# A linear-attention and MLP block on one core: the second pair's w2 and attention as one product by seven products, its output transposed and summed on GpSimd

## The chip, the cores and the metric

The kernel runs on one core of a Trainium2 chip. A core has TensorE for matrix products (PE in the profile; PEld is its loading of weights), VectorE (DVE), ScalarE (ACT), GpSimd (POOL) and SyncE (SP), which here only issues DMA transfers. SBUF is the core's memory with 128 partitions, PSUM the memory into which TensorE writes; GpSimd computes from and to SBUF. The metric is the device time of one execution in microseconds (us), the median of the runs.

## The reference

Everything is float32, 2048 tokens of 512 channels, 32 heads of 16, 1376 hidden channels.

```python
xn = layernorm(x)                                  # over the 512 channels
q, k, v = split(xn @ wqkv)                         # [512, 1536]
pq, pk = phi(q), phi(k)                            # phi(t) = where(t > 0, t + 1, exp(t)) + 1e-6
kv, z = einsum("bhsd,bhse->bhde", pk, v), pk.sum(tokens)
attn = (pq @ kv) / (pq . z + 1e-6) @ wo            # wo: [512, 512]
h = relu(xn @ w1 + b1) ** 2                        # w1: [512, 1376]
out = x + attn + h @ w2 + b2                       # w2: [1376, 512]
```

## The kernel before, in words

**Products in three passes.** Each float32 operand is split into a high part (a copy by ACT, which rounds to float32r) and a low part (what is left, a subtraction by DVE of two SBUF operands: `split`, L122, `rest_of`, L125). A product is three matmuls: high x high, high x low, low x high (`PASSES`, `three`, L133). All tiles have 128 partitions; a matmul's weights are 128 x 128 and it streams 512 or 256 columns.

**Tokens.** The 16 tiles of 128 tokens make four blocks of 512 tokens. A first loop over the tiles normalises x, transposes it and builds k and the sum over tokens (`kx`, L398). From it comes `m`, the matrix by which phi(q) goes into the output (kv times wo). Then the loop `for n in range(2)` (L1060) takes the token blocks in two pairs: blocks 3 and 2 (t1, t2) in the first pair, 1 and 0 in the second.

**Places.** Per pair, q and w1 are worked off in seven "places" (`order`: two for q, five for w1), each of which makes 2 x 128 output channels for both blocks of the pair. A place is a 2 x 2 product of blocks made with seven block products instead of eight (`product`, L498: six matmuls of 512 columns each): the operands on the weights' side are the quarters A11, A12, A22 and the sums S1 to S4 of quarters (`chunk_sums`, L736, on DVE), split into parts by `chunk_split` and `last_split` into the tiles `aop`; on the tokens' side they are the transposed x (`xs`) and its differences (`T`). The banks A, before, B and C of PSUM hold the block products; ACT copies and DVE adds bring them together.

**After a place.** For w1 the results go through relu (L486) and a square to a hidden tile, which is split (`hidden_2`) and multiplied by its 128 rows of w2 (`mlp_2`, 12 matmuls) for t1 in between the products of the next places, and for t2 after the places. For q, `steps_of` turns phi(q) and divides by its sum on ACT and DVE. In the first pair attention is added with `add_attention` (12 matmuls for 128 tokens), in the second by `Seven`: block products of 256 columns (L1046) with sums made by DVE. The last 96 hidden channels go as two 128-row matmuls and one 32-row matmul for a tile of tokens (`last_2`, `quarters_2`).

**Output.** The output of 128 tokens is a bank of 512 columns; DVE adds it to the tile `res` (L1178), which holds x and, through an adding DMA on POOL's queue, b2; SP stores it.

**Order.** The program's order on each engine is as the code records it; how many of the waiting steps are taken at a point of a place is in tables (`AT`, `AE`, `TM`). SP's queue is worked off in order. Rings set reuse: tag "p" has six tiles of 512 columns, tag "raw" six for loads.

Of the kernel before, what the change touches and what calls it, by code (L numbers as in the profile page):

```python
# [10 lines left out]
OP = mybir.AluOpType  # L11
# [7 lines left out]
def kernel(  # L19
# [400 lines left out]

    def steps_of(t, j, done=False, parts=False):
# [8 lines left out]
        def weighted():  # L430
            pz = w512(f"pz{t}_{j}", "p", 6)
            tiles.append(pz)
            nc.scalar.activation(pz, o, AF.Identity, bias=zc[:, 1, j:j + 1], scale=zc[:, 0, j:j + 1])  # L433

        def sums():
            pt = w512(f"pt{t}_{j}", "p", 6)
            den = small.tile([P, H], F32, name=f"dt{t}_{j}", tag="den")
            nc.vector.transpose(blocks(pt), blocks(tiles[0]))
            nc.vector.tensor_reduce(den, heads_of(pt), axis=AX.X, op=OP.add)
            tiles.append(den)  # L440
# [534 lines left out]
    def matrix_sums(stage):  # L975

        t = [two(f"mr{r}") for r in range(2)]
        for r in range(2):
            nc.gpsimd.dma_start(t[r], md[:, 2 * r:2 * r + 2])
# [7 lines left out]
        def high(x, h, to, at):  # L987
            copy("act", h.bitcast(F32R), x)
            nc.gpsimd.dma_start(mtd[0][:, to, at], h)

        def low(x, h, to, at):
            nc.vector.tensor_tensor(out=x.bitcast(F32R), in0=x, in1=h, op=OP.subtract)
            nc.gpsimd.dma_start(mtd[1][:, to, at], x)
# [6 lines left out]
    class Seven:  # L1000

        def __init__(self, t, pairs=range(2)):
            self.t = t
            self.at = [slice(r * BT // 2 + pairs[0] * P, r * BT // 2 + (pairs[-1] + 1) * P) for r in range(2)]
            self.o = [[q[t][:, 2 * c:2 * c + 2, at] for c in range(2)] for at in self.at]

        def sums_o(self):

            (a11, a12), (a21, a22) = self.o
            return [lambda: self.op(a22, a21, a22, OP.add), lambda: self.op(a21, a11, a21, OP.subtract),  # L1010
                    lambda: self.op(a11, a22, a11, OP.subtract), lambda: self.op(a12, a12, a11, OP.subtract)]

        def op(self, o, x, y, how):
            nc.vector.tensor_tensor(out=o, in0=x, in1=y, op=how)

        def load_m(self):

            self.mt = both("mt", ("xs0h", "xs0l"))
            for o, src in zip(self.mt, mtd):
                nc.gpsimd.dma_start(f32(o), src)  # L1020

        def parts(self, src, to, order):

            highs, lows = [], []
            for c, at in order:
                h, l, x = (a[:, 2 * c:2 * c + 2, at] for a in (*to, src))
                highs.append(lambda h=h, x=x: copy("act", h, x))
                lows.append(lambda h=h, l=l, x=x: rest_of(l, x, h))
            return highs, lows

        def parts_o(self):

            self.s = both(f"so{self.t}", ("xs1h", "xs1l"))
            one, two = self.at
            return self.parts(q[self.t], self.s, ((1, one), (0, one), (0, two), (1, two)))

        def run(self, ps, left, right, e, first=False):

            c, r = left[1:]
            for i in range(2):  # L1040
                for n, (u, v) in enumerate(PASSES):
                    at = slice(r * (BT // 2) + e * P, r * (BT // 2) + (e + 1) * P)
                    a = aT[self.t, 2 * c + i][:, u, at] if left[0] == "a" else self.s[u][:, 2 * c + i, at]
                    w, k, z = right
                    b = (m if w == "m" else self.mt)[v][:, 2 * k + i, z]
                    nc.tensor.matmul(ps, lhsT=a, rhs=b, start=first and i == 0 and n == 0, stop=False,  # L1046
                                     skip_group_check=True)

        def into(self, ps, k, a):

            r = res[self.t, k][:, a]
            if a != LO and a != HI:
                r, ps = r.rearrange("p (a z) -> p a z", a=2), ps[:, None, :].to_broadcast([P, 2, D // 2])
            nc.vector.tensor_tensor(out=r, in0=ps, in1=r, op=OP.add)

    ALL = slice(0, D)

    last = TB - 1
    res = {}
    for n in range(2):  # L1060
        t1, t2 = NB - 1 - 2 * n, NB - 2 - 2 * n
        x1, x2 = xsb
        tag = "acc" if n else "ps"

        order = [("q", 0), ("w", 0), ("q", 1), *(("w", k) for k in range(1, NP))]
        NO = len(order)

        AT = (((0, 0, 0, 0, 0, 0, 0, 0, 0),
# [14 lines left out]
               (0, 0, 0, 0, 0, 0, 0, 2, 0)))[n]  # L1083
        AE = ((3, 1, 2, 3, 5, 2, 0, 1, 4, 5, 2),
              (2, 3, 2, 2, 0, 0, 0, 0, 0, 0, 0))[n]
        TM = {(1, 0): 4, (1, 4): 2, (1, 6): 1, (2, 4): 2, (3, 7): 1, (3, 0): 1, (4, 7): 1} if n else {}

        def matrix_step(p, at):
            do(m_sums, TM.get((p, at), 0))

        steps = {t1: [], t2: []}
        r2 = [work.tile([P, k, 512], F32, name=f"r2{u}{n}", tag=f"r{u}") for u, k in zip("abc", (4, 4, 3))]
        waiting = [*range(NF - 2, -1, -1), NF - 1]
        r2 = {f: r2[k // 4][:, k % 4] for k, f in enumerate(waiting)}
        m_sums = matrix_sums([r2[f] for f in waiting[:4]]) if n else []

        def last_units(rz):
            nc.scalar.activation(rz, rz, AF.Square)
            sz, rests = hidden_last(f"sz{n}", rz)

            def packed():
                lqs.append(quarters(f"sz{n}", rz, sz[0], work, "heads"))

            return sz, rests, packed

        lqs = []

        if n == 0:

            more()  # L1110
            pz2 = bank("pz0b")
            plain_1(pz2, z, x2)
            more()

            rz = r2[1]
            relu(rz, pz, NF - 1)
            relu(r2[NF - 1], pz2, NF - 1)
            do(extra, 2)
            values()
            do(extra, len(extra))  # L1120
        else:
            w2next = []
            pz = bank(f"pz{n}", "acc")
            plain_1(pz, z, x1)
        q.update({t1: four(f"q{t1}", "r2"), t2: four(f"q{t2}", "r1")})
        attention_places("r3", "r0")
        w = load_1(*order[1])
        s = {}
        if n:
            rz = w512(f"rz{n}", "p", 6)  # L1130
            relu(rz, pz, NF - 1)
            sz, sz_rests, packed = last_units(rz)
            sz_rests()
            packed()

        w2order = [NF - 1, *range(NF - 1)]

        def next_2(t):

            do(w2next, 2 - highs.pop(0))  # L1140
            if t + 1 < NF and (n == 0 or t >= TB - 1):
                f = w2order[t + 1]
                w2next.extend(piece_2(f, place(f)))

        def high_2():
            do(w2next)
            highs[0] = 1

        highs = [0] * NF
        if n:  # L1150
            next_2(0)


        banks = [bank(f"b{n}_{k}") for k in range(4)]
        t5, biased = None, []

        def load_res(t):
            for k in range(2):
                r = two(f"res{t}_{k}")
                i = t * TB + 2 * k  # L1160
                nc.sync.dma_start(r, xf[i * P:(i + 2) * P, :].rearrange("(i p) d -> p i d", i=2))
                for i in range(2):
                    res[t, 2 * k + i] = r[:, i, :]
                biased.append(r)

        def add_bias():

            def to(r):
                for i in range(2):
                    nc.gpsimd.dma_start(r[:, i], b2[None, :].partition_broadcast(P), accum_op=OP.add)  # L1170

            todo = [lambda r=r: to(r) for r in biased]
            biased.clear()
            return todo
# [420 lines left out]
```

## Time and profile before

| | us |
|---|---|
| median of 3 runs (407.48 to 408.0) | 407.62 |
| the profiled execution's span | 406.3 |
| PE busy | 401.3 |
| DVE busy | 329.2 |
| ACT busy | 273.3 |
| POOL busy | 57.3 |
| DMA moved | 55.31 MB, mean 136 GB/s |

The span runs from the first to the last instruction of the profiled execution; the time of a run also holds what lies around it. Busy time of an engine is the union of its instructions. A matmul's row in the profile is longer than the distance to the next one, because matmuls overlap; what one costs in a chain of them is the distance. "PEclk" is the clock that TensorE was granted, in tenths, DMA "share" the mean busy share of the 16 DMA engines.

### The profile page before, as it was taken

How to read it: one execution, taken by the hardware profiler on the slowest of the kernel's cores; microseconds unless marked ns; L12 is line 12 of the kernel's file. 1: busy time of each engine (PE TensorE's matmuls, PEld its weight loads, DVE VectorE, ACT ScalarE, POOL GpSimd, SP SyncE). 2: the span in 40 equal slices, each digit the busy share in tenths (PEclk: the TensorE clock that was granted, in tenths of full speed). 3: DMA queues.
4: the chain of work that ended last, by engine and by line, in shares of the span. 5: the costliest groups of instructions: out<-in, count | busy, mean ns of one | idle time of the engine just before them, and what ended most of it. 6: DMA issues, size and time to landing. Idle time of an engine off the chain costs nothing.

```text
span 406.3 us, 5887 instructions
## 1 busy us (share of the span) xinstructions
PE 401.3 (99%) x2011; PEld 334.1 (82%) x2011; DVE 329.2 (81%) x603; ACT 273.3 (67%) x478; POOL 57.3 (14%) x93
## 2 busy tenths in 40 slices
PE   8999999999999999999999999999999999999996
PEld 7888888888788888888878888888888888888895
DVE  5886666497898999988349998598989688989983
ACT  5777777456788789887728751578678857957430
POOL 5444333220000000030000300102200013000300
PEclk9999999999999999999999999999999999999999
DMA  5857656820463231291563912824331739306512
GB/s 210 275 166 230 208 157 205 241 45 0 121 193 80 77 103 27 85 224 29 186 231 124 227 38 91 231 53 129 122 113 52 207 110 305 53 34 224 105 26 105
DMA packets 48623, 55.31 MB, mean 136 GB/s; under 512 B 8593, under 2 KB 31377, under 8 KB 48082
## 3 DMA queue, kind: packets, MB, share of 16 engines
q1 hardware_dynamic: 44994, 45.50, 36.4%
q0 software_dynamic: 3520, 9.44, 9.9%
q8 instruction: 16, 0.26, 0.3%
q14 instruction: 13, 0.11, 0.1%
q10 hardware_dynamic: 80, 0.00, 0.0%
HBM read 40.90 MB, written 12.85 MB: 132 GB/s over the span
## 4 chain that ended last, share of the span: by engine, by line
PE 97%; DMA 1%; DVE 1%; ACT 0%; issue 0%
PE b L498 33%; PE acc L133 32%; PE pk L378 11%; PE kx L398 11%; PE acc L1046 2%; PE acc L509 2%; PE pz L133 1%; PE x L1046 1%; PE xl L1046 1%; DMA x<-in_A_x_dram 1%; PE b L133 1%; PE pz0b L133 1%; PE pt L310 0%; PE yl L1046 0%; PE y L1046 0%; PE acc L516 0%
## 5 line engine op out<-in xcount | busy, mean ns | idle before, releaser
L133 PE MATMUL acc<-w2r,s 128*128 128x512 f32 x477 | 113.0, 390 | 0.0
L133 PEld LDWEIGHTS acc<-w2r,s 128*128 128x128 f32 x477 | 89.3, 188 | 19.0 <-issue 0.7
L498 PE MATMUL b<-T,aop 128*128 128x512 f32 x336 | 83.5, 390 | 0.0
L498 PEld LDWEIGHTS b<-T,aop 128*128 128x128 f32 x336 | 63.0, 188 | 13.9 <-ACT t L114 0.8
L398 PE MATMUL kx<-pk,tok 128*128 128x512 f32 x192 | 46.0, 390 | 0.0
L398 PEld LDWEIGHTS kx<-pk,tok 128*128 128x128 f32 x192 | 36.0, 188 | 7.6 <-ACT pk L114 0.2
L1170 POOL DMA_DIRECT2D res<-in_B_b_dram x16 | 14.4, 1038 | 173.6 <-DVE S L736 85.9
L498 PE MATMUL b<-xs0h,aop 128*128 128x512 f32 x112 | 36.9, 391 | 0.0
L114 ACT ACTIVATE aop<-S 128x512 fp32r<-128x512 f32 x28 | 17.5, 624 | 13.1 <-DVE S L736 13.1
L359 POOL TENSOR_TENSOR tok<-xp,tok 128x512 fp32r<-128x512 f32 x15 | 19.8, 1320 | 39.8 <-ACT tok L114 39.8
L498 PEld LDWEIGHTS b<-xs0h,aop 128*128 128x128 f32 x112 | 21.0, 188 | 4.4
L125 DVE TENSOR_TENSOR w2r<-r,w2r 128x512 fp32r<-128x512 f32 (+2 forms) x35 | 23.8, 683 | 0.7 <-ACT w2r L114 0.6
L114 ACT ACTIVATE w2r<-r 128x512 fp32r<-128x512 f32 x32 | 19.6, 618 | 6.1 <-PE acc L133 4.7
L122 DVE TENSOR_TENSOR aop<-S,aop 128x512 fp32r<-128x512 f32 x28 | 19.3, 689 | 4.5 <-ACT aop L114 4.1
L498 PE MATMUL b<-xs0l,aop 128*128 128x512 f32 x56 | 21.8, 389 | 0.0
L122 DVE TENSOR_TENSOR s<-c,s 128x512 fp32r<-128x512 f32 x20 | 13.6, 689 | 7.6 <-ACT s L114 7.4
L498 PE MATMUL b<-xs1h,aop 128*128 128x512 f32 x56 | 19.5, 389 | 0.0
L114 ACT ACTIVATE T<-Tf 128x512 fp32r<-128x512 f32 x16 | 9.5, 625 | 14.4 <-DVE Tf L679 14.3
L114 ACT ACTIVATE c<-b 128x512 f32<-128x512 f32 x28 | 16.4, 585 | 2.8 <-PE b L498 2.6
L433 ACT ACTIVATE pz<-q,zc 128x512 f32<-128x512 f32 x16 | 12.9, 808 | 6.3 <-DVE q L419 6.3
L1178 DVE TENSOR_TENSOR res<-acc,res 128x512 f32<-128x512 f32 x16 | 10.5, 688 | 7.9 <-PE acc L133 5.1
L369 ACT ACTIVATE k<-pk 128x512 f32<-128x512 f32 x16 | 9.5, 593 | 9.7 <-PE pk L378 9.5
(265 smaller groups left out, 853.8 us busy)
## 6 DMA issues: line engine op xcount, KB each, us to landing
r<-in_B_w_dram SPq DMA_DIRECT2D x49, 256.0 KB, 3.5
res<-in_A_x_dram SPq DMA_DIRECT2D x8, 512.0 KB, 4.7
res<-in_B_b_dram POOLq DMA_DIRECT2D x16, 256.0 KB, 5.8
out_dram<-res SPq DMA_DIRECT2D x15, 256.0 KB, 2.1
via<-xp SPq DMA_DIRECT2D x5, 512.0 KB, 2.6
xg<-via SPq DMA_DIRECT2D x20, 128.0 KB, 2.8
xTd<-t SPq DMA_DIRECT2D x8, 256.0 KB, 3.4
x<-in_A_x_dram SPq DMA_DIRECT2D x4, 512.0 KB, 4.4
```

What stands on the lines that cost most here:

```text
L114: nc.scalar.activation(o, i, AF.Copy, bias=bias)
L122: ENG[el].tensor_tensor(out=l, in0=src, in1=f32(h), op=OP.subtract)
L125: nc.vector.tensor_tensor(out=l, in0=src, in1=f32(h), op=OP.subtract)
L133: nc.tensor.matmul(ps, lhsT=a[u], rhs=b[v], start=first and n == 0, stop=last and n == 2)
L359: ENG[el].tensor_tensor(out=l, in0=src, in1=f32(h), op=OP.subtract)
L378: nc.tensor.matmul(ps, lhsT=cols(i)[u][:, j, slot(i)], rhs=w[v][:, j, :], start=first and n == 0, stop=last and n == len(steps) - 1)
L398: nc.tensor.matmul(kxp[c], lhsT=tok[i][:, u, c * P:(c + 1) * P], rhs=pk[i][:, v], start=i == 0 and (u, v) == first, stop=i == NT - 1 and ( ...
L433: nc.scalar.activation(pz, o, AF.Identity, bias=zc[:, 1, j:j + 1], scale=zc[:, 0, j:j + 1])
L498: nc.tensor.matmul(ps, lhsT=a[u][:, j * P:(j + 1) * P], rhs=b[v][:, j, :], start=first and j == 0 and n == 0, stop=last and j == 1 and n == 2,
L1046: nc.tensor.matmul(ps, lhsT=a, rhs=b, start=first and i == 0 and n == 0, stop=False, skip_group_check=True)
L1170: nc.gpsimd.dma_start(r[:, i], b2[None, :].partition_broadcast(P), accum_op=OP.add)
L1178: nc.vector.tensor_tensor(out=r[:, a:z], in0=ps, in1=r[:, a:z], op=OP.add)
```

## The change

The loop over pairs is written out as two pieces of code. The first pair's computation is as before; beside it each place stores its split operands to DRAM (`keep_operands`). Since w1 and wq are the same for both pairs, the second pair loads these parts (`load_operand`, two places ahead) instead of loading w1, summing and splitting it again.

In the second pair the hidden activations h and phi(q) together form the rows of one product: 7 chunks of 128 channels in each half (5 of h, 2 of attention), for the two blocks of tokens. That 2 x 2 product (tokens x halves of the channels, by halves of the channels x halves of the output) is made by seven block products M1 to M7 after all seven places are done; no w2 matmul stands between the places any more. Six of them give the output transposed: weights are w2's parts with every second column (`columns`), 512 tokens stream. The sums on the w2 side are made by POOL during the places (`first_parts`), stored, and loaded again as parts are needed; the sums on the left side (`sum_of`) are made by POOL for h and by DVE for attention; squares of h are POOL's too (`square`). A finished product is turned back in blocks of 32 x 32 by DVE (`turned_out`) and added to `res` by POOL (`into`). M3, the seventh, is made in rows of tokens with 256 columns. The core of the diff:

```diff
-            nc.gpsimd.dma_start(t[r], md[:, 2 * r:2 * r + 2])
+            nc.sync.dma_start(t[r], md[:, 2 * r:2 * r + 2])
...
-    class Seven:
...
+    def keep_operands(p, *which):
+        for s in which:
+            src = aop[s // 2][:, s % 2]
+            nc.sync.dma_start(aopd[p][s], f32(src[:, :, p % 2 * 256:][:, :, :256] if s == 3 else src))
...
+    def square(o, x, f):
+        relu(x, x, f)
+        nc.gpsimd.tensor_tensor(out=o, in0=x, in1=x, op=OP.mult)
...
+        def sums():                                   # in first_parts(k): the sums of two chunks of w2
+            t3.append(ends[:, 2, LO])
+            for out, x, y in ((t3[0], b22, b12), (b12, b12, b11), (b22, b22, b12), (b21, b21, b22)):
+                nc.gpsimd.tensor_tensor(out=out, in0=x, in1=y, op=OP.subtract)
...
+    rings = {"units": [("B0", "A0", "A1"), 0], "singles": [(1, 4, 0), 0]}
+    def unit(name, src):
+        t = unit_tile(name)
+        split(t[:, 0], t[:, 1], src, "act", "dve")
+        return [[t[:, u, i] for u in range(2)] for i in range(2)]
...
+    def combine(eng, to, x, y, how, *which):
+        for part in which:
+            o, a, b = (source(rc, part) for rc in (to, x, y))
+            ENG[eng].tensor_tensor(out=o, in0=a, in1=b, op=how)
...
+    def mul(name, ps, *which, first=False):
+        for part in which:
+            for a, b in zip(half_units[name, part], rights(name, part)):
+                for e in range(2):
+                    for n, (u, v) in enumerate(PASSES):
+                        nc.tensor.matmul(ps[e], lhsT=columns(b[u], e, None), rhs=a[v],
+                                         start=first and n == 0, stop=False, skip_group_check=True)
...
+    def into(r, half, tiles, es=range(2), eng="pool"):
+        for e in es:
+            o = res[r, half].rearrange("p a n -> p (a n)").rearrange("p (b c e) -> p e b c", e=2, c=Q)[:, e]
+            ENG[eng].tensor_tensor(out=o, in0=by_blocks(tiles[e]), in1=o, op=OP.add)
...
+    sum_of(1, "pool", 0, 1, 2)
+    mul("M4", X, 1, 2)
+    left("M1", 0, 1, 2)
+    sum_of(3, "pool", 0, 1, 2)
+    mul("M1", Ac, 0, 1, 2, first=True)
...
+    left("M2", 0, 1, 2)
+    sum_of(2, "pool", 0, 1, 2)
...
+    into(0, 0, m1)
+    into(1, 0, m4)
+    mul("M2", Bc, 0, 1, 2, "q", first=True)
+    left("M6", 0, 1, 2, "q")
...
+    sum_of(4, "pool", 0, 1, 2)
...
+    mul("M7", Y, 0, 1, 2, "q", first=True)
+    left("M3", 0, 1, 2, "q")
```

Parts 0 and 1 of a left side are two chunks of h each (1024 elements in a partition), part 2 is the fifth chunk (512), part "q" attention's two (1024). The three "units" of the ring hold split left parts in turn.

What that makes of two engines' order after the last place. First POOL (GpSimd). Before, after the operands of the second pair, its last rows are DMA issues (`mth`, `mtl`: the summed matrix m, `res`: adding b2):

```order
L1020 DMA mth_3238<-mthd_1069 128x2048
L1020 DMA mtl_3239<-mtld_1070 128x2048
L1170 DMA res1_0_3075<-in_B_b2_dram 128x512 x2
L1170 DMA res1_1_3077<-in_B_b2_dram 128x512 x2
L1170 DMA res0_0_3613<-in_B_b2_dram 128x512 x2
L1170 DMA res0_1_3615<-in_B_b2_dram 128x512 x2
```

After, the rows that follow the first block sum (`h01`: the block of the second half of the channels for t1; `h4`: a fifth chunk):

```order
L1666 TENSOR_TENSOR res1_3371<-M1t1_3456,res1_3371 128x512
L1666 TENSOR_TENSOR res10_3136<-M4t0_3463,res10_3136 128x512
L1666 TENSOR_TENSOR res10_3136<-M4t1_3467,res10_3136 128x512
L1551 TENSOR_TENSOR h01_2649<-h01_2649,h00_2648 128x1024 x2
L1551 TENSOR_TENSOR h4_2652<-h4_2652 128x512
L1666 TENSOR_TENSOR res1_3371<-M2t0_3551,res1_3371 128x512
L1666 TENSOR_TENSOR res1_3371<-M2t1_3553,res1_3371 128x512
L1666 TENSOR_TENSOR res10_3136<-M6t0_3618,res10_3136 128x512
L1666 TENSOR_TENSOR res10_3136<-M6t1_3620,res10_3136 128x512
```

POOL's DMA issues of this stage are gone, and sums of blocks and additions to `res` stand in their place, the fourth block sum behind the first four additions.

Second DVE (VectorE) in the same stage. Before, it splits hidden tiles and w2 (`s`, `w2r`) and takes attention through its steps:

```order
L122 TENSOR_TENSOR s1_0_3_3638<-r2b1_2496,s1_0_3_3638 128x512
L125 TENSOR_TENSOR w2r0_1020<-r2_3_3376,w2r0_1020 128x512
L444 TENSOR_SCALAR dt0_3_3620<-dt0_3_3620 128x32
L445 RECIPROCAL dt0_3_3620<-dt0_3_3620 128x32
L446 STREAM_TRANSPOSE pz0_3_3617<-dt0_3_3620 128x512
L449 SCALAR_TENSOR_TENSOR q0_2516<-q0_2516,pz0_3_3617 128x512
L122 TENSOR_TENSOR aTsr0_3526<-q0_2516,aTsr0_3526 128x512
```

After, around the left and right parts of M2 and M6:

```order
L122 TENSOR_TENSOR M2_0_3423<-h01_2649,M2_0_3423 128x1024
L122 TENSOR_TENSOR M2_1_3426<-h01_2649,M2_1_3426 128x1024
L122 TENSOR_TENSOR M2_2_3429<-h4_2652,M2_2_3429 128x512
L125 TENSOR_TENSOR rightM6_3435<-T2r0_3257,rightM6_3435 128x2x256
L125 TENSOR_TENSOR rightM6_3435<-T2r2_3259,rightM6_3435 128x2x256
L125 TENSOR_TENSOR xs1l_77<-T2r4_3261,xs1l_77 128x256
L1551 TENSOR_TENSOR q0_2556<-q0_2556 128x1024
L1551 TENSOR_TENSOR q0_2556<-q1_2555,q0_2556 128x1024
L1659 STREAM_TRANSPOSE M1t0_3452<-M1b0_3450 128x512
L1659 STREAM_TRANSPOSE M1t1_3456<-M1b1_3454 128x512
L122 TENSOR_TENSOR M2_q_3458<-q1_2555,M2_q_3458 128x1024
```

The splits of left parts are now 1024 elements wide and made once for each of the seven products, and the turning back of a product stands between the parts of the next.

More of the change, by code (lines that the diff above doesn't have):

```diff
@@ L998, in matrix_sums @@
                                                               (low, 1), (low, 2), (low, 3)))]
-    class Seven:
[L1002 to L1054, printed above, removed]
@@ new lines @@
+    AE = (3, 1, 2, 3, 5, 2, 0, 1, 4, 5, 2)
+    steps = {t1: [], t2: []}
+    r2 = [work.tile([P, k, 512], F32, name=f"r2{u}", tag=f"r{u}") for u, k in zip("abc", (4, 4, 3))]
+    waiting = [*range(NF - 2, -1, -1), NF - 1]
+    r2 = {f: r2[k // 4][:, k % 4] for k, f in enumerate(waiting)}
+    lqs = []
+    more()
+    pz2 = bank("pz0b")
+    plain_1(pz2, z, x2)
+    more()
+    rz = r2[1]
+    relu(rz, pz, NF - 1)
+    relu(r2[NF - 1], pz2, NF - 1)
+    do(extra, 2)
+    values()
+    do(extra, len(extra))
@@ new lines @@
+            product(C, S1, [T[1][:, u] for u in range(2)], True)
+            keep_operands(p, 2)
+            t5_ = w512(f"t5_{p}", "p", 6)
+            copy("act", t5_, C)
+            step(at_p[1])
+        else:
+            do(bias, 2)
+            mlp_2(acc, pa, s.pop(pa))
+        if was:
+            product(before, A22b, [T[4][:, u] for u in range(2)], False, True)
+            if was == "w":
+                c21 = w512(f"c21_{p}", "p", 6)
+                relu(c21, before, pb)
+            elif p == 1:
+                copy("dve", q[t1][:, pb], before)
+            else:
+                phi_T(q[t1][:, pb], before)
+                steps[t1] += steps_of(t1, pb, True, True)
@@ new lines, with second_sums @@
+        if kind == "w":
+            high_2()
+        if p == 0:
+            last_sums(4, difference_high, difference_low)
+        if kind == "w":
+            relu(r2[fa], c12, fa)
+        else:
+            steps[t2] += steps_of(t2, fa)
+        step(at_p[5])
+        if kind == "w" and fa:
+            next_2(fa + 2)
+        def second_sums(f=pb, first=not was):
+            if first:
+                for k in range(TB):
+                    last_2(acc[k], k, sz, True, False)
+            else:
+                mlp_2(acc, f, s.pop(f))
@@ new lines @@
+    do(prepare, len(prepare))
+    step(len(steps[t2]))
+    do(parts_2, NJ)
+    first_loads()
+    for k in range(TB):
+        add_attention(acc, t2 * TB + k)
+        if k == 0:
+            columns_low(x2, f2)
+            for f in reversed(last_two):
+                wait_for(f)
+            columns_low(x1, f1)
+    second_loads()
+    for k in range(TB):
+        for j, f in enumerate(last_two):
+            sum_2(acc[k], k, f, j == 1)
+        add(acc[k], t2, k)
+        store(t2, k)
+    t1, t2 = NB - 3, NB - 4
```

1062 lines of the change are left out of this document (619 added, 443 removed), and 21 rows, old and new, of the table AT.

## The prediction, made before the changed kernel was run

> **What bounds the kernel now.** I read the page first: the busy line, the granted clock, and the chain that ended last.
>
> ```profile
> PE 401.3 (99%) x2011; PEld 334.1 (82%) x2011; DVE 329.2 (81%) x603; ACT 273.3 (67%) x478; POOL 57.3 (14%) x93
> PEclk9999999999999999999999999999999999999999
> PE 97%; DMA 1%; DVE 1%; ACT 0%; issue 0%
> ```
>
> PE is the bound from end to end, at full clock: 97% of the chain is matmuls. DVE has 81% of the span, POOL only 14%. Then the busy time by stage, for the second pair: its seven places, and what follows them in the changed program (PE's time 322 is worked out below).
>
> ```profile
> 251.30:322.00 70.70, 70.70 (x313) 58.53 (x312) 59.13 (x112) 50.96 (x91) 6.88 (x10) 1.00 0.46 139
> 322.00:402.60 80.60, 80.60 (x444) 69.86 (x442) 68.43 (x126) 47.61 (x84) 8.16 (x10) 1.00 0.43 119
> ```
>
> The columns are length, PE, PEld, DVE, ACT, POOL, clock, DMA share, GB/s. PE has no gap in either row, so a matmul less is time less, as long as nothing else makes PE wait. DVE stands at 84% and 85%: it is the engine next in line. POOL computes nothing here; its busy time is DMA issues.
>
> The price of a matmul comes from the chain in order of time (start, length, what, count), and the ends from PE's and DVE's timelines.
>
> ```profile
> 284.56 9.52 PE b L498 x42
> 386.70 4.29 PE acc L1046 x36
> 208.18 0.40 PE L516 MATMUL acc<-w2q,s0q 32*128 32x512 f32 x4
> 208.51 0.73 PE L133 MATMUL acc<-w2r,s 128*128 128x512 f32 x2
> 251.28 0.39 PE L133 MATMUL pz<-xs0h,w1z 128*128 128x512 f32 x1
> 402.24 0.40 PE L509 MATMUL end<-w2r,s 128*128 128x256 f32 x2
> 402.67 0.42 DVE L1178 TENSOR_TENSOR res<-end,res 128x256 f32<-128x256 f32 x1 [0.17 <-PE end L509]
> ```
>
> A matmul of 512 columns costs 9.52/42 = 0.227 us, one of 256 columns 4.29/36 = 0.119, four of 32 rows together 208.51 - 208.18 = 0.33. The second pair starts on PE at 251.28. PE ends at about 402.6, and 3.7 us of add and store follow to the span's 406.3. The median of the runs, 407.62, is 1.3 above this execution; I add that at the end.
>
> **The change, part by part.** *PE.* Before, the second pair's w2 and attention take 251 matmuls of 512 columns, 178 of 256 and two sets of four 32-row ones. After: six products of 7 chunks x 2 channel halves x 3 passes = 252, and 12 for the last channels, 264 of 512; the seventh, in rows of tokens, 84 and 8 more, 92 of 256; six wide and four narrow 32-row ones, about the old 0.7 us. That is 13 x 0.227 - 86 x 0.119 = -7.3 us. The seven places keep their 294 matmuls. So PE could stand at 251.28 + 2.72 (last channels) + 48 x 0.227 (place 0) + 6 x 9.52 = 322.0 when the last stage starts.
>
> *Parts of w1 kept in memory.* The first pair gains 28 stores of 12.8 MB on SP's queue, each behind the split that makes its data and ahead of loads made two places early; the parts are overwritten a place later. Cost 0; without that cover a late w1 load would cost its landing, 3.5 us by the row below. In exchange the second pair makes no w1 sums and splits, and loads 49 pieces of 256 KB instead, each issued two places (19 us) before its use.
>
> ```profile
> 335.00:345.00 10.00, 10.00 (x46) 8.29 (x45) 8.75 (x15) 7.93 (x14) 3.38 (x5) 1.00 1.01 308
> r<-in_B_w_dram SPq DMA_DIRECT2D x49, 256.0 KB, 3.5
> ```
>
> From the second pair's start to the loads of its last place, SP issues 15.2 MB in some 49 us, 310 GB/s; with its share at 1.01 the DMA moved 308. So the loads run at the limit and fall a few us behind, inside the 19 us of lead: 0, or up to 4 if a store that waits for POOL holds SP's queue.
>
> *Places of the second pair.* The 24 mlp matmuls that stood between the products of a w1 place go, so a place is 9.52 us instead of some 15. DVE's work there: 60 operations of 0.65, 16 transposes of 0.70, 8 reductions of 0.69, 16 small ones: 60 us in 68, against 59.1 in 70.7 before; POOL gets 15 squares and 20 quarter sums. PE can wait 18 x 0.227 = 4 us (three products) for an add before it needs its bank again. Bounds 0 and 5, I take 1.
>
> *The last stage, on which the sum turns.* Here DVE splits each product's left and right parts (a subtraction of two SBUF operands each), and POOL makes the sums of the blocks and adds the turned outputs to res, also from SBUF. What the two do to each other the trace shows where POOL already computes: POOL's rows, then DVE's.
>
> ```profile
> 24.26 1.62 POOL L359 TENSOR_TENSOR tok<-xp,tok 128x512 fp32r<-128x512 f32 x1 [1.13 <-ACT tok L114]
> 40.79 1.30 POOL L359 TENSOR_TENSOR tok<-xp,tok 128x512 fp32r<-128x512 f32 x1 [3.91 <-ACT tok L114]
> 83.31 1.34 POOL L359 TENSOR_TENSOR tok<-xp,tok 128x512 fp32r<-128x512 f32 x1 [4.47 <-ACT tok L114]
> 88.53 1.29 POOL L359 TENSOR_TENSOR tok<-xp,tok 128x512 fp32r<-128x512 f32 x1 [3.85 <-ACT tok L114]
> ...
> 24.07 0.66 DVE L386 SCALAR_TENSOR_TENSOR pk<-k,pk 128x512 fp32r<-128x512 f32 x1
> 40.84 0.70 DVE L295 STREAM_TRANSPOSE t<-xg 128x512 f32<-128x512 f32 x1
> 80.15 0.69 DVE L701 TENSOR_TENSOR wv<-wv,wvl 128x512 f32<-128x512 f32 x1 [2.50 <-DMA wvl<-in_A_wqkv_dram]
> 83.41 1.79 DVE L701 TENSOR_TENSOR wv<-wv,wvl 128x512 f32<-128x512 f32 x1
> 88.58 1.79 DVE L701 TENSOR_TENSOR wv<-wv,wvl 128x512 f32<-128x512 f32 x1
> ```
>
> The same L701 takes 0.69 us alone and 1.79 when it starts just after a POOL operation: it does nothing until POOL is done. At 24.26 it is the other way round: POOL takes 1.62 instead of 1.30 since DVE was in a two-operand step. The transpose at 40.84, with one operand, is not touched. So I take it that a POOL operation and a DVE operation with two SBUF operands exclude each other, and add up their times as if they stood on one engine. The Trainium skill ("SBUF — State Buffer", Who interferes with whom) says it as a rule: a VectorE instruction with two SBUF inputs and a GpSimd one that reads SBUF share a port that is locked for a whole instruction, and whoever comes first blocks the other. Without the rule one could put the two 1.79 down to chance and leave the last stage at PE's own time; by the rule it always happens. The rows above agree with it.
>
> The durations, each with its back-to-back spacing:
>
> ```profile
> 31.27 1.30 POOL L359 TENSOR_TENSOR tok<-xp,tok 128x512 fp32r<-128x512 f32 x1 [0.75 <-ACT tok L114]
> 32.51 0.10 POOL L348 MEMSET xp<- 128x1 f32 x1
> 238.93 1.29 DVE L125 TENSOR_TENSOR T<-Tf,T 128x512 fp32r<-128x512 f32 x2
> 240.14 2.35 DVE L125 TENSOR_TENSOR xs1l<-xT,xs1h 128x1024 fp32r<-128x1024 f32 x2
> 394.62 1.48 DVE L1054 TENSOR_TENSOR res<-xl,res 128x256 f32<-128x256 f32 x4
> L438 DVE STREAM_TRANSPOSE pt<-pz 128x512 f32<-128x512 f32 x16 | 11.3, 704 | 0.0
> L1207 DVE TENSOR_TENSOR t<-b,t 128x512 f32<-128x512 f32 x10 | 6.8, 685 | 0.0
> L486 ACT ACTIVATE c<-c,b1s 128x512 f32<-128x512 f32 x10 | 7.2, 722 | 6.0 <-DVE c L1228 6.0
> ```
>
> POOL: 1.24 us for 512 elements; for 1024, not in the trace, twice that. DVE: 0.65 for 512, 1.18 for 1024, 0.37 for 256. From the start of the last stage to the last left part of the seventh product (M3_q), DVE has 23 two-operand steps of 1024, 17 of 512, 5 of 256: 27.0 + 11.0 + 1.9 = 39.9 us. POOL has the four block sums, 4 x (2 x 2.48 + 1.24) = 24.8, and ahead of the last product's own 14 additions to res, 17.4. Together 82.1. PE needs in that time 270 x 0.227 + 0.7 + 1.1 + 15 x 0.119 = 64.8. DVE's 12 transposes before M3_q (8.4) can lie beside POOL.
> Upper end: all 82.1 in turn, after the 2.6 us in which nothing can start (add 0.69, relu 0.72, POOL's square 1.24): 82.1 + 2.6 - 64.8 = 20. Lower end: DVE always goes first, and of POOL's work only what M3's parts need counts (block sums, and the 4 additions that POOL has ahead of the fourth): 39.9 + 24.8 + 5.0 + 2.6 - 64.8 = 7.5. The trace has no case in which both queues are full, so I take the middle, 14. Behind it nothing changes: after M3_q PE has 69 x 0.119 = 8.2 us, then an add and a store as before. ACT (47.6 of 80.6 us before, and fewer copies after) is not late.
>
> Six products read their weights with a step of two elements. No row shows such a load; the plain one takes 0.188 beside a matmul of 0.227, so it costs nothing, or, at twice the length, 270 x 0.15 = 40.
>
> ```profile
> L498 PEld LDWEIGHTS b<-T,aop 128*128 128x128 f32 x336 | 63.0, 188 | 13.9 <-ACT t L114 0.8
> ```
>
> I take 0. Sum: 406.3 - 7.3 + 1 + 14 = 414.0, and 415.3 with the 1.3 to the median.
>
> **The rivals.** *PE stays gapless* and the change is faster: 406.3 - 7.3 + 1.3 = 400.3. For it speaks that PE waits for nobody today; against it the two 1.79 rows and the 82.1 us against 64.8. It decides if exclusion costs less than 7.3 us. *The port at its worst, and places that wait too* (DVE full, operand loads behind): 20 + 5, 425. For it: 60 of 68 us on DVE, and 310 against 308 GB/s; against it the 19 us of lead. *Strided weights at half speed*: 440 or more; only the absence of a row speaks for it.
>
> **How the numbers follow.** A measurement tells 0.2% (0.8 us) from no change. Port decides, 408.5 to 422: 0.70, most likely 415. Beyond that (places, loads, weights): 0.08. Exclusion mostly hidden, 399 to 408.4: 0.22, of which 0.02 lands within 0.2%; the first case gives another 0.01 there. So faster 0.20, same 0.03, slower 0.77. The range 401 to 425 leaves out about 0.1 below and 0.08 above; the likeliest case alone is 408.5 to 422.
>
> **What would show it.** In the profile after: PE without a gap up to about 322, then idle before the split products, its weight loads waiting for DVE's subtractions (M1, M2, M6 first). DVE's 1024-element subtractions of 1.2 us at 2 to 3.5 us where POOL is busy, POOL's sums above 2.5; transposes still 0.70. The matmuls at 0.227 and 0.119 as now. I am wrong if DVE's mean there stays near 1.2, if POOL takes far less than 2.48 for 1024 elements, or if PE waits for DMA instead.

## The result

The changed kernel takes 437.94 us (median of 4 runs, 437.82 to 439.54), the kernel before 407.81 on the same chip: 1.075 times as long, interval 1.0731 to 1.0768. I had said 415.3, at most 425. The profiled execution spans 436.1 us (before 406.3), so 29.8 us are to be found.

The page of the changed kernel: busy time, granted clock by slices, and the chain that ended last.

```profile
PE 407.2 (93%) x1940; PEld 330.6 (76%) x1940; DVE 348.0 (80%) x523; ACT 262.1 (60%) x440; POOL 137.7 (32%) x138
PEclk9999999999999999999999999999989998996999
PE 63%; DVE 13%; DMA 8%; issue 7%; ACT 4%; POOL 4%; SPq 0%; DVEq 0%; POOLq 0%; ACTq 0%
```

PE was 97% of the chain and is 63%; DVE, DMA, ACT, POOL and time for which the profile shows no wait ("issue") share the rest, so there are several waits. PE's timeline gives the borders: the first matmul of the second pair, the first of the last stage, and the last of all. Then the busy time between them (length, PE, PEld, DVE, ACT, POOL, clock, DMA share, GB/s).

```profile
254.14 0.39 PE L133 MATMUL pz<-xs0h,w1z 128*128 128x512 f32 x1
334.33 2.96 PE L1610 MATMUL x<-M,w2r 128*128 128x512 f32 x12
431.13 0.28 PE L133 MATMUL end<-mh,M_q 128*128 128x256 f32 x1
...
254.14:334.33 80.19, 74.91 (x314) 59.01 (x312) 65.17 (x100) 50.48 (x84) 30.11 (x33) 0.98 0.86 265
334.33:431.40 97.07, 82.11 (x373) 66.15 (x371) 84.25 (x66) 36.81 (x53) 64.85 (x33) 0.95 0.35 85
```

Against my sum: the second pair starts at 254.14 instead of 251.28 (+2.9); its places take 80.2 us where I had 70.7 without gaps (+9.5, I had allowed 1); the last stage takes 97.1 where PE needs 64.8 + 8.2 = 73.0 (+24.1, I had allowed 14); the tail is 4.7 instead of 3.7 (+1.0). With the -7.3 of PE's count that is 30.2; the 0.4 above 29.8 lies in that count, which by the trace is 80.6 - 73.0 = 7.6. These are the stages of one execution: in the nine profiles here whose places are the same, the places take 77.6 to 82.4 us.

**First pair.** The chain, ACT's and PE's timelines, and the stretch in which it happens:

```profile
105.20 6.77 DMA aop_0d<-aop
112.07 0.63 ACT L114 ACTIVATE aop<-r 128x512 fp32r<-128x512 f32 x1 [3.02 <-DMA aop_0d<-aop]
113.24 1.65 PE L503 MATMUL b<-T,aop 128*128 128x512 f32 x6 [2.58 <-ACT c L114]
108.00:112.00 4.00, 2.66 (x12) 1.86 (x10) 1.20 (x2) 1.05 (x2) 0.00 (x0) 1.00 1.05 399
```

The copy that writes the next place's parts into `aop` waits for the store that still reads the old ones, 6.77 us long while the DMA is full (share 1.05). Behind it in ACT's queue stands the copy of a bank (`c`) for which PE waits.

**Places.** PE's four waits of over 0.5 us, then what stands behind the last of them on POOL and ACT, and the granted clock around it:

```profile
281.95 1.66 PE L503 MATMUL b<-T,S 128*128 128x512 f32 x6 [1.33 <-DVE d L1440]
293.03 4.38 PE L503 MATMUL b<-T,slot 128*128 128x512 f32 x18 [1.07 <-DVE q L1779]
303.73 1.66 PE L503 MATMUL b<-T,S 128*128 128x512 f32 x6 [0.80 <-DVE d L1440]
319.86 0.50 PE L503 MATMUL b<-xs1h,slot 128*128 128x512 f32 x1 [2.04 <-ACT d L114]
...
315.47 0.74 POOL L1482 TENSOR_TENSOR h<-w2p 128x256 f32<-128x256 f32 x1 [4.86 <-DMA w2p<-in_B_w_dram]
318.69 0.63 ACT L114 ACTIVATE xs1l<-w2p 128x512 fp32r<-128x512 f32 x1 [3.37 <-POOL w2p L1482]
...
317.60:319.80 2.20, 0.22 (x1) 0.00 (x0) 1.06 (x2) 1.11 (x3) 1.98 (x3) 1.00 1.03 349
319.80:322.20 2.40, 2.31 (x7) 1.34 (x7) 2.40 (x3) 2.37 (x6) 1.21 (x1) 0.67 0.77 268
322.20:324.50 2.30, 2.30 (x6) 1.86 (x7) 1.18 (x3) 2.22 (x4) 1.04 (x1) 0.60 0.66 131
```

The first three are DVE's lateness. The fourth starts with a late load of a quarter of w2: POOL waits 4.86 us for it, ACT's copy waits for POOL, and the copy of a bank queues behind that. PE's 2.04 us without matmuls are then followed by 4.7 us at a granted clock of 0.67 and 0.60.

**Last stage.** Four groups of DVE and POOL from 334 on (busy us, mean ns), PE's four longest waits, and the clock after the longest:

```profile
L122 DVE TENSOR_TENSOR M<-h,M 128x1024 fp32r<-128x1024 f32 x12 | 22.6, 1916 | 0.7 <-ACT M L114 0.7
L125 DVE TENSOR_TENSOR rightM<-b21r,rightM 128x512 fp32r<-128x512 f32 x2 | 5.7, 2884 | 0.0
L1659 DVE STREAM_TRANSPOSE M6t<-a 128x512 f32<-128x512 f32 x2 | 1.3, 684 | 0.0
L1551 POOL TENSOR_TENSOR h<-h,h 128x1024 f32<-128x1024 f32 x8 | 23.8, 2989 | 0.0
...
343.37 1.43 PE L1610 MATMUL x<-M,xs1h 128*128 128x512 f32 x5 [1.68 <-DVE M L122]
346.70 4.23 PE L1610 MATMUL a<-M,w2r 128*128 128x512 f32 x17 [1.67 <-DVE M L122]
365.46 6.96 PE L1610 MATMUL b<-M,rightM 128*128 128x512 f32 x23 [2.94 <-DVE M L122]
397.65 8.06 PE L1610 MATMUL a<-M,rightM 128*128 128x512 f32 x24 [6.18 <-DVE M6t L1659]
...
397.65:405.55 7.90, 7.90 (x25) 6.37 (x26) 7.90 (x8) 1.06 (x1) 7.05 (x4) 0.69 0.82 188
```

The two steps of 512 elements (`rightM`) take 2.88 us instead of 0.65, the steps of 1024 on average 1.92 instead of 1.18; transposes keep 0.68. The longest wait is that of M5's product, whose bank comes free only when DVE has turned M6 out. After M5 PE has no gap any more. One by one, where both queues are full, the two engines alternate:

```profile
347.76 3.38 POOL L1551 TENSOR_TENSOR h<-h,h 128x1024 f32<-128x1024 f32 x1
348.80 2.89 DVE L122 TENSOR_TENSOR M<-h,M 128x512 fp32r<-128x512 f32 x1
351.10 2.85 POOL L1551 TENSOR_TENSOR h<-h,h 128x1024 f32<-128x1024 f32 x1
351.61 3.42 DVE L122 TENSOR_TENSOR M_q<-q,M_q 128x1024 fp32r<-128x1024 f32 x1
```

POOL's operation of 351.10 ends at 353.95, and DVE's, begun at 351.61, 1.08 later at 355.03: it did its 1.1 us only then.

### The profile page after: what moved, and what is told of

The parts are those of the page before. It is cut to its first block, busy times and chain, and to the rows that moved or that the text cites. A ratio compares the mean times of both kernels' runs of the same rounds, so it can differ in the third digit from the quotient of the medians.

```text
span 436.1 us, 5899 instructions
## 1 busy us (share of the span) xinstructions
PE 407.2 (93%) x1940; PEld 330.6 (76%) x1940; DVE 348.0 (80%) x523; ACT 262.1 (60%) x440; POOL 137.7 (32%) x138
## 4 chain that ended last, share of the span: by engine, by line
PE 63%; DVE 13%; DMA 8%; issue 7%; ACT 4%; POOL 4%; SPq 0%; DVEq 0%; POOLq 0%; ACTq 0%
PE acc L133 18%; PE b L503 15%; PE pk L378 10%; PE kx L398 10%; DVE M L122 4%; PE a L1610 3%; PE end L133 2%; PE y L1610 2%; POOL w2p L1482 2%; DMA w2p<-in_B_w_dram 2%; DMA b21r<-in_B_w_dram 2%; DMA aop_0d<-aop 2%; DVE rightM L125 1%; DVE M_q L122 1%; PE pz L133 1%
## 5 line engine op out<-in xcount | busy, mean ns | idle before, releaser
L133 PE MATMUL acc<-w2r,s 128*128 128x512 f32 x240 | 56.9, 390 | 0.0
L133 PEld LDWEIGHTS acc<-w2r,s 128*128 128x128 f32 x240 | 45.0, 188 | 9.7 <-issue 0.4
L503 PE MATMUL b<-T,aop 128*128 128x512 f32 x168 | 42.0, 391 | 2.6 <-ACT c L114 2.6
L122 DVE TENSOR_TENSOR M<-h,M 128x1024 fp32r<-128x1024 f32 (+1 forms) x23 | 36.8, 1639 | 6.5 <-ACT M L114 6.5
L503 PEld LDWEIGHTS b<-T,aop 128*128 128x128 f32 x168 | 31.3, 188 | 10.3 <-ACT c L114 3.0
L114 ACT ACTIVATE M<-h 128x1024 fp32r<-128x1024 f32 (+1 forms) x23 | 18.6, 845 | 22.4 <-PE a L1610 20.9
L1551 POOL TENSOR_TENSOR h<-h,h 128x1024 f32<-128x1024 f32 (+1 forms) x10 | 27.6, 2790 | 0.0
L503 PE MATMUL b<-T,slot 128*128 128x512 f32 x96 | 24.6, 403 | 1.1 <-DVE q L1779 1.1
L503 PEld LDWEIGHTS b<-T,slot 128*128 128x128 f32 x96 | 18.5, 195 | 6.2 <-DVE q L1779 1.5
L503 PE MATMUL b<-T,S 128*128 128x512 f32 x72 | 19.0, 399 | 2.1 <-DVE d L1440 2.1
```

Source lines behind the costliest of these rows:

```text
L114: nc.scalar.activation(o, i, AF.Copy, bias=bias)
L122: ENG[el].tensor_tensor(out=l, in0=src, in1=f32(h), op=OP.subtract)
L133: nc.tensor.matmul(ps, lhsT=a[u], rhs=b[v], start=first and n == 0, stop=last and n == 2)
L503: nc.tensor.matmul(ps, lhsT=a[u][:, j * P:(j + 1) * P], rhs=b[v][:, j, :], start=first and j == 0 and n == 0, stop=last and j == 1 and n == 2,
L1551: ENG[eng].tensor_tensor(out=o, in0=a, in1=b, op=how)
```

## The experiments

Unless said otherwise each is one edit of the changed kernel, so it is read against 437.9. Gains are differences of medians.

**1. No POOL work in the last stage.**

```diff
-            ENG[eng].tensor_tensor(out=o, in0=a, in1=b, op=how)
+            if eng != "pool":
+                ENG[eng].tensor_tensor(out=o, in0=a, in1=b, op=how)
...
-            ENG[eng].tensor_tensor(out=o, in0=by_blocks(tiles[e]), in1=o, op=OP.add)
+            pass
```

> POOL's work of the last stage is left out: the block sums and the additions of the turned products to res (so the output lacks them). Theory A (POOL and DVE exclude each other, and that made the last stage 24 us longer than PE's own 73): without POOL the stage falls to 73-79 us, the kernel to 414-420, DVE's 1024-element subtractions to 1.2 us. Rival (DVE's own queue, in which PE's next operands stand behind transposes and splits, sets the stage): DVE's list is unchanged, so under 8 us come back, 430 or more.

418.0 us (ratio to before 1.023, 1.0189 to 1.0271): 20.0 come back. The group of DVE and PE's whole last stage:

```profile
L122 DVE TENSOR_TENSOR M<-h,M 128x1024 fp32r<-128x1024 f32 x12 | 14.5, 1219 | 6.7 <-ACT M L114 6.6
336.14:412.40 76.26, 76.26 (x372) 63.77 (x371) 52.16 (x66) 36.83 (x53) 2.74 (x2) 1.00 0.46 109
```

The same subtractions take 1.22 us, PE has no gap, the clock is 1.00. With POOL's work the last stage is 97.1 - 76.3 = 20.8 us longer. The rival falls.

**2. Which part of POOL's work.** In one run only the block sums are left out (the first edit above), in another only the additions to res (the second).

> Of POOL's work in the last stage only the block sums are left out (four sums over five blocks each); the additions to res stay on POOL. If what the port costs goes by POOL's time (42.2 us in all by my own terms, 24.8 of them sums, and 20 us came back for all of it), 12 us come back: 426 (424-428). If the sums cost more than their share, because they stand where DVE's first splits are waited for by PE, 14 to 18: 420-424.

> The other half: the additions of the turned products to res are left out, the block sums stay on POOL. By POOL's time 8 us come back: 430 (428-432). If only sums matter (the additions lie beside transposes and behind PE's own work), 2 to 5: 433-436.

Without the sums 418.1 us (ratio 1.0259, 1.023 to 1.0289), without the additions 431.2 (1.0579, 1.0563 to 1.0594). The sums alone give back all of the 20, more than either of the two values expected. The additions give back 6.7, inside the range by share of time (428 to 432). The two parts, 26.5 together, do not add to 20. Is it the place of the sums, at the head of the stage, or their length? One run leaves out the first two sums only, one puts those two on DVE (shown), one all four:

```diff
-    sum_of(1, "pool", 0, 1, 2)
+    sum_of(1, "dve", 0, 1, 2)
...
-    sum_of(3, "pool", 0, 1, 2)
+    sum_of(3, "dve", 0, 1, 2)
```

> Only the first two block sums are left out (10 operations of POOL, 12.4 us of its own time, at the head of the last stage); the other two and the additions to res stay on POOL. If the head decides (DVE's first splits wait there, and all that follows is late), 13 to 18 of the 20 us come back: 420-425. If it goes by length, half, 428.

> All work done: the first two block sums on DVE, the other two and the additions on POOL. If the head decides, close to the run with four sums on DVE, within 3 us of it. If not, half way between it and the changed kernel's 437.9.

> All work done: the four block sums on DVE (12 us more there), the additions to res on POOL as in the changed kernel. DVE has 39.9 + 12 + 8.4 = 60 us before the last left part, and POOL's additions 17.4 beside it cost little while DVE has air (run without the sums): 420-425, against 428.3 with the additions on DVE too. If DVE is full with the sums, each addition on POOL blocks it longer (1.24 us) than it would take on DVE (0.65): 428-433.

Two sums left out: 426.8 (1.0459, 1.0442 to 1.0477), 11.2 back. Two on DVE: 433.2 (1.0626, 1.061 to 1.0641), half way between four on DVE and the changed kernel. Four on DVE: 428.9 (1.054, 1.0479 to 1.0601), in the range for a full DVE. It goes by length, not by the head.

**3. Everything on DVE.** Sums and additions on DVE (with the squares on ACT too: experiment 7).

```diff
-            ENG[eng].tensor_tensor(out=o, in0=a, in1=b, op=how)
+            nc.vector.tensor_tensor(out=o, in0=a, in1=b, op=how)
...
-            ENG[eng].tensor_tensor(out=o, in0=by_blocks(tiles[e]), in1=o, op=OP.add)
+            nc.vector.tensor_tensor(out=o, in0=by_blocks(tiles[e]), in1=o, op=OP.add)
```

> The same work is done, but the block sums and the additions to res stand on DVE, none on POOL. Theory A: DVE gets 12 us of sums and 9 of additions more, but no longer waits for POOL; to the last left part it has 39.9 + 12 + 9 + 8.4 = 69 us against PE's 65, so the stage takes 78-86 us and the kernel 419-427. Rival (POOL's operations cost DVE little, DVE is simply the longer list): 10 to 20 us slower than the changed kernel, 446 or more.

428.3 us (1.0517, 1.0458 to 1.0577): 9.6 better, as exclusion asks, though 1.3 above the range. PE still waits for M6's turn:

```profile
390.81 7.38 PE L1610 MATMUL a<-M,rightM 128*128 128x512 f32 x24 [3.21 <-DVE M6t L1659]
```

**4. What the alternation must wait for.** PE's first M5 matmul needs everything that DVE has in its queue up to M6's turn, and what POOL puts between. In the run without POOL, PE goes from the stage's first matmul to M5 in 45.2 us, and DVE is busy for 34.7 of them; the changed kernel needs 63.3 for the same 194 matmuls:

```profile
336.14:381.30 45.16, 45.16 (x194) 36.10 (x192) 34.70 (x43) 25.90 (x38) 2.74 (x2) 1.00 0.45 113
334.33:397.65 63.32, 48.36 (x194) 36.88 (x192) 59.38 (x42) 27.02 (x40) 46.47 (x22) 0.96 0.30 75
```

With POOL at work DVE's own operations take 59.4 us instead of 34.7, and it is idle for only 3.9 (without POOL, for 10.5). So it is held inside its operations; waiting for POOL's results, the other way for POOL to make it late, does not add to its idle time.

So I add DVE's 34.7, the block sums (24.8 on POOL by the prediction's durations, 12.0 on DVE) and the six additions before M5 (7.4 on POOL, 3.9 on DVE) as on one engine and take off 45.2. Beside it stands each run's median less the 418.0 without POOL work:

| last stage | list to M6's turn | over 45.2 | measured |
|---|---|---|---|
| as changed | 34.7 + 24.8 + 7.4 = 66.9 | 21.7 | 20.0 |
| two sums on DVE | 34.7 + 6.0 + 12.4 + 7.4 = 60.5 | 15.3 | 15.3 |
| no additions | 34.7 + 24.8 = 59.5 | 14.3 | 13.2 |
| first two sums out | 34.7 + 12.4 + 7.4 = 54.5 | 9.3 | 8.8 |
| four sums on DVE | 34.7 + 12.0 + 7.4 = 54.1 | 8.9 | 10.9 |
| all on DVE | 34.7 + 12.0 + 3.9 = 50.6 | 5.4 | 10.4 |
| no sums | 34.7 + 7.4 = 42.1 | 0 | 0.1 |

The list, made after the runs, is right within 2 us but for the last but one: with all on DVE 5 us more are lost. The trace of that run shows what the list leaves out. Up to M5 DVE is busy for 48.6 us of 54.8 and idle for 6.2, in three waits for ACT's copies. ACT's copy ahead of the longest one (2.97 us, before 359.53) had itself waited 3.1 us for PE's matmuls.

**5. No store of place 0.**

```diff
-        for s in which:
+        for s in which if p else ():
...
+        kept = aopd[p or 2][s]
```

> The first place of the first pair keeps no operands (the second pair's first place loads those of the third, so its values are others). Theory C (the ACT copy that overwrites the parts waits 3 us for the store of place 0): 3.0 us come back, 434.9. Rival (the parts of place 1 are late for another reason, the load behind them): 437.9, and ACT's wait of 3 us only changes its name.

434.6 us (1.0657, 1.064 to 1.0675), 3.3 back: theory C holds. ACT's copy no longer waits, and the second pair starts at 250.72:

```profile
108.41 0.63 ACT L114 ACTIVATE aop<-r 128x512 fp32r<-128x512 f32 x1
250.72 0.39 PE L133 MATMUL pz<-xs0h,w1z 128*128 128x512 f32 x1
```

Where the store is kept, the second pair starts anywhere from 253.8 to 256.7 in the profiles of these runs; in the three without it, from 250.7 to 251.9. PE's wait behind the store is 2.0 to 3.1 us, and the clock adds the larger part of the spread (0.62 instead of 1.00 for 4.5 us, as after the 2.21 us in the profile with the squares on ACT, is 1.7 us): in the five profiles in which it stays at 1.00 after the wait the pair starts by 254.3, in the eight in which it falls, at 255.1 or later.

In the profile of this run 0.8 of the 3.4 us gained at the start of the pair are left at the start of the last stage (333.51 for 334.33). Its time of 435.98 is the longest of the four, so the 3.3 rests on the medians.

**6. Operands loaded for two places only.**

```diff
+        if p >= 2:
+            held_ops[p][name] = held_ops[p - 2][name]
+            return
```

> The second pair loads the operands of its first two places only; later places use those again (other values), 9 MB less on the DMA while the places run. Theory B (the DMA at its limit makes w2's parts land late, ACT and POOL queue behind them, and the last block squares wait for a store): 4 to 8 us come back, 430-434, most of them between 310 and 345 us. Rival (DVE's list alone holds the places): under 1.5 us, 436.5 or more.

433.6 us (1.0629, 1.06 to 1.0658), 4.3 back, the low end of theory B. The DMA's share in the middle of the places, changed kernel and then this run, and POOL's wait for the fourth quarter, which had been 4.86 us:

```profile
264.00:310.00 46.00, 42.80 (x183) 33.76 (x183) 40.31 (x63) 32.10 (x53) 17.35 (x19) 1.00 0.82 258
```

```profile
264.00:310.00 46.00, 44.47 (x190) 35.07 (x190) 38.53 (x64) 31.91 (x53) 16.97 (x19) 1.00 0.36 117
311.03 0.92 POOL L1485 TENSOR_TENSOR h<-w2p 128x256 f32<-128x256 f32 x1 [0.23 <-DMA w2p<-in_B_w_dram]
```

The wait behind ACT is gone, and PE's three waits for DVE shrink to 0.41 to 0.58 us. The places take 75.3 us in this profile.

**7. Fewer sums of w2's quarters; squares on ACT.**

```diff
-            for out, x, y in ((t3[0], b22, b12), (b12, b12, b11), (b22, b22, b12), (b21, b21, b22)):
+            for out, x, y in ((t3[0], b22, b12),):
...
-        nc.gpsimd.tensor_tensor(out=o, in0=x, in1=x, op=OP.mult)
+        nc.scalar.activation(o, x, AF.Square)
```

> In the second pair's places POOL makes one of the four sums of a quarter of w2 instead of four (the parts kept are then others); loads and stores stay. Theory A in the places (15 operations of 0.75 us of POOL hold DVE's two-operand steps, and DVE is full there): 2 to 4 us come back, 434-436. Rival B (the DMA alone sets when a quarter lands, and who waits for it): under 1 us.

> The 15 squares of h go from POOL to ACT, which has 58 of 91 us busy there; all else as in the changed kernel. Theory A: POOL's 17 us fall away from the port in the places and the block sums of the last stage start some 2 us earlier: 433-436. Rival: the places wait for DMA and for DVE's own list, and ACT's queue gets 10 us longer: 437-440.

One sum instead of four: 435.3 (1.0672, 1.0654 to 1.069), 2.7 back, so POOL's sums cost in the places too: DVE's same 100 operations take 60.8 us instead of 65.2. In its profile the places fall from 80.2 to 74.3 us. But the second pair starts 2.6 us later than in the changed kernel's, at 256.70, and the last stage is 1.0 longer, at a clock of 0.91 instead of 0.95.

```profile
256.70:330.96 74.26, 73.39 (x313) 57.99 (x312) 60.77 (x100) 50.21 (x84) 17.74 (x18) 1.00 0.87 274
330.96:429.00 98.04, 84.58 (x373) 67.64 (x371) 84.11 (x66) 36.99 (x53) 64.32 (x33) 0.91 0.37 95
```

Squares on ACT: 436.9 (1.0714, 1.0698 to 1.073), only 1.1 back, between the two expectations: ACT still stands behind POOL's sums (2.99 us at 320.34), and PE's longest waits are now for ACT's copies instead of DVE's adds. Together with all on DVE:

> All of the work done, the least of it on POOL: block sums and additions to res on DVE, squares on ACT. If the two add, 428.3 - 1.1 = 427 (425-428.5). If DVE, full at the head of the last stage, takes the squares' gain away, 428-430. Neither comes near the kernel before.

428.1 us (1.0503, 1.0476 to 1.0531), the same as without; it lies in both ranges and does not tell the two apart. With 428.3 and 428.9 (four sums on DVE) it is the best that does all of the work, 20 us behind the kernel before.

**8. Contiguous weights**, on top of the first edit, where PE has no gaps.

```diff
-        return at.rearrange("p (c e) -> p e c", e=2)[:, e]
+        return at.rearrange("p (e c) -> p e c", e=2)[:, e]
```

> As the run without POOL in the last stage (418.0 us, PE without a gap there), and the weights of the six products are read as contiguous columns (so the output's channels stand in another order). In that run 24 matmuls took 5.70 us, 0.2375 each, instead of 0.227. If the step of two elements does it, they take 5.45 here and the kernel 415-416.5; if not, 5.6-5.7 as before and 417.5-418.5.

414.6 us (413.5 to 417.0) against 418.0 (414.4 to 418.2): the spreads overlap. The profiles tell more, with the step of two first:

```profile
369.93 5.86 PE L1611 MATMUL a<-M,rightM 128*128 128x512 f32 x24
375.63 1.56 PE L1611 MATMUL a<-M,xs1l 128*128 128x512 f32 x6
```

```profile
369.97 5.73 PE L1611 MATMUL a<-M,rightM 128*128 128x512 f32 x24
375.54 1.52 PE L1611 MATMUL a<-M,xs1l 128*128 128x512 f32 x6
```

From start to start 24 matmuls take 5.70 us, and 5.57 contiguous: 0.005 each, about half of what I looked for. That would be 1.4 us for the 264; the whole last stage is 1.0 shorter in these two profiles (76.6 and 75.6). The rest of the distance to 24 x 0.227 = 5.45 has another cause, which I have not found.

**9. The cuts together**: 1, 5 and 6, and then 7 (the sums) and 8 as well.

> Three cuts at once: no POOL work in the last stage, no store of place 0, operands loaded for two places only. If the three losses are independent, their gains add: 437.9 - 20.0 - 3.3 - 4.3 = 410.3 (409-412). If one is hidden behind another, or a new wait takes its place, 413 or more.

> The three cuts together (409.7 us) with two more: three of the four quarter sums of w2 left out, and contiguous weights. If both are still exposed, 2.7 and 1.0 us come back: 406 (404.5-407.5), some 6 above the 400.3 of a PE without gaps. If the quarter sums only cost through the DMA that is gone already, 408-409.

409.7 us (1.0048, 1.0032 to 1.0064) and 406.2 (0.9969, 0.9948 to 0.9991). In the medians the three gains add (expected 410.3), and so do the other two (406). In the profiles those of the places do not: they are 4.9 us shorter with fewer loads, 5.9 with fewer sums and 6.2 with all five edits, so in part it is one loss that either removes. With all five out, much of the work missing, the kernel is 1.5 us faster than before. Its stages:

```profile
251.36:325.31 73.95, 72.99 (x314) 58.17 (x313) 60.14 (x100) 50.38 (x84) 18.47 (x18) 1.00 0.53 161
325.31:401.30 75.99, 75.70 (x373) 62.09 (x371) 51.29 (x67) 36.95 (x53) 2.04 (x2) 1.00 0.48 118
```

That is 3.3 and 3.0 above the 70.7 and 73.0 of PE without gaps; the second pair starts where it did before.

## Why the prediction was wrong

The direction was right, and its reason; the size was not. Three terms of the sum failed: the last stage (14 in the sum, 24.1 measured), the places (1 and 9.5) and the stores of the first pair (0 and 2.9). The miss of 22.6 us by steps, from the profiled execution (the runs' gains beside it):

| step | predicted | measured | shown by |
|---|---|---|---|
| PE's count | -7.3 | not seen by itself: with five cuts the second pair is still 6.3 above it | 9 |
| stores of the parts, first pair | 0 | 2.9 | 5: 3.3 back |
| places (with operand loads) | 1, at most 5 | 9.5 | 6: 4.3, 7: 2.7 back |
| last stage | 14, at most 20 | 24.1 | 1: 20.0 back |
| strided weights (in the last stage) | 0 | 1.0 to 1.4 | 8, by one profile of each |
| tail | 0 | 1.0 | not tried |

- *"The parts are overwritten a place later. Cost 0."* This step failed. A store is a reader too: ACT's next write waits for it, and at place 0, where the DMA is full (share 1.05), it takes 6.8 us. The price that I named for a lost cover, 3.5 us, was about right, but I gave it to a late load.
- *"Inside the 19 us of lead: 0, or up to 4."* The operand loads were indeed hidden: PE's waits in the places are for DVE and ACT. The 308 GB/s was not the most that the DMA moves (399 from 108.00 to 112.00), and over the places it moved 265 GB/s. But on the same full queue stand the loads of w2's quarters, one buffer through which load, sums and stores follow each other without lead. They came late; cutting the operand loads gave back 4.3.
- *"I take 1"* for the places rested on DVE's sum of 60 us in 68 and on PE's slack of 4 us. It left out that the exclusion, which I used for the last stage, holds here as well (experiment 7: 2.7 back, and 4.4 us less of DVE's time), and that ACT's copies can queue behind POOL.
- *The last stage:* mechanism right, size wrong, and outside my own bounds. The step that failed is the point at which I compared. I put 82.1 us of port work up to M3's last part against 64.8 us of PE. The point that decides is earlier: before M5 there stand all four sums, six additions, most of the splits and eight of the transposes (66.9 us) against 45.2 of PE. I also let the transposes lie beside POOL. But M6's turn stands behind three subtractions in DVE's queue and began at 396.80, when these ended after 4.75 us. My middle between the ends had no ground: the alternation in the trace is close to the end where everything goes in turn. A slip besides: the 0.65 for 512 elements is a row's length by its count; the spacing is (240.14 - 238.93)/2 = 0.605, which takes some 0.8 off the 39.9.
- *The clock* was in no term. It is 0.95 over the last stage: about 5 us of the 97 (0.05 x 97), an estimate. The loss comes with PE's long waits, the 2.94 us ahead of 365.46 (0.78 for the 6.8 us behind it) and the 6.18 ahead of 397.65 (0.69 for 7.9). The run without POOL shows it only as part of the same 20.
- Of the signs that I named these came: DVE's subtractions at 1.9 to 2.9 us, POOL's sums at 2.99, transposes at 0.68. These did not: PE without a gap up to 322 (it waits at 113.24 and four times in the places), and matmuls at 0.227 (0.2375 in the last stage, without POOL's work too). The rival without gaps (400.3) is far off; that of the port at its worst with waiting places (425) named the port and waiting places, which is right, and was still 13 short; strided weights are not what brought the time near 440.
- The Trainium skill's rule ("SBUF — State Buffer", Who interferes with whom) that the one which comes later waits for the other's whole instruction agrees with the alternation at 347.76 to 355.03.

## What to carry to other kernels

Put POOL's operations and DVE's two-operand ones on one list, in their order, and compare it with PE's work at every point where PE needs a result or a bank, not at the end of the stage. Count a store as the last reader of its tile, and on a full queue look for the chain with a single buffer, not for the largest loads. Where PE is the bound, moving work from it onto engines that are 80% busy pays only as far as those engines are free at that place.

## What the runs showed of the hardware

- With both queues full, POOL and DVE alternate one for one in the changed kernel (from 347.76): a DVE step of 512 elements takes 2.89 us, one of 1024 takes 3.42 (alone 0.65 and 1.22). A short step is almost as dear as a long one. It does not always go one for one: in the run with two sums on DVE a sum of POOL begun at 348.63 took 7.66 us, while DVE did six two-operand steps at their own length, without a gap, from 349.54 to 353.98.
- One kind of DVE step with a single operand is held as well: a 128x32 `TENSOR_SCALAR`, 0.17 us alone, that starts just after a square of POOL ends with it. POOL's row, then DVE's:

```profile
305.50 1.04 POOL L1437 TENSOR_TENSOR h<-d 128x512 f32<-128x512 f32 x1 [1.84 <-ACT d L491]
305.57 1.01 DVE L449 TENSOR_SCALAR dt<-dt 128x32 f32<-128x32 f32 x1
```

- How long PE waits does not settle by itself whether the clock falls. After the 2.04 us ahead of 319.86 it was 0.67 and 0.60 for 4.7 us; after the 2.58 us ahead of 113.24, in the same execution, it stayed at 1.00, and so it did after the 1.67 us ahead of 346.70. At the place of the 2.58 the run with squares on ACT waited 2.21 us and its clock fell (six matmuls in 2.20 us instead of 1.65):

```profile
113.32 2.20 PE L503 MATMUL b<-T,aop 128*128 128x512 f32 x6 [2.21 <-ACT c L114]
```

  In all profiles here, from 20 us on, no wait of 1.0 to 1.68 us made the clock fall, of those from 1.69 to 2.65 some did and some did not, and every one from 2.84 us did. The Trainium skill ("TensorE: Matmul & The Clock Gate", Part 1: The HAM clock gate) has the clock fall after an idle window of about 3.4 us. Here waits of 1.7 to 2.7 us were enough in some cases, so the measurement decides.
- Stores of 512 KB beside loads: the DMA moved 399 GB/s at a share of 1.05.
